# Windowed attention feeding an MoE-style block on one Trainium2 core: a written-out list of due times, and a planner that counts transfers

## The chip, the cores and the metric

The kernel runs on one core of one Trainium2 chip. The core has TensorE (matmuls; PE in the profile, PEld for its weight loads), VectorE (DVE), ScalarE (ACT), GpSimd (POOL), SyncE (SP, which here only issues transfers), and 16 DMA engines that all queues share. Each engine has its own in-order instruction queue. The metric is device microseconds of one execution; lower is better.

## The reference, cut to what matters

Attention over q, k, v of shape (4 batches, 8 heads, 768 positions, 64 wide), in which a query sees the first 8 positions and the last 96, with a bias that falls with distance; then a block on the 3072 tokens of 512 values.

```python
scores = scale * q @ k.T                         # per head, scale 1/8
keep   = is_global | is_local                    # first 8 keys, or 0 <= i - j < 96
scores = where(keep, scores + bias, -1e9)        # bias = -slope[h] * distance
a      = exp(scores - max); a = a / sum(a)
x      = (a @ v) as (B*S, H*D)                   # 3072 x 512

h    = x @ w_in                                  # 512 -> 1024
solu = h * softmax(h)
ln   = (solu - mean) / sqrt(var + 1e-6) * g_ln
out  = ln @ w_out                                # 1024 -> 512, fp32
```

## The kernel before, in words

The work is cut into steps. A batch's attention goes by pairs of heads (4 pairs a batch). For each pair, `k` and `q` are loaded in fp32 (`load_rows`, L338 to L347), cast to fp16 on POOL (for batch 0 also on ACT; L515), transposed by TensorE into PSUM (L523, L528) and evicted into `kT` and `qT` (L544 to L556). Batches 0 and 1 load "big" rows, in which a partition takes several neighbouring positions, 2 KB of `k` or 1.5 KB of `q` in one run; batches 2 and 3 load one position per run, 256 B. The big form needs a reordering eviction. `v` is always loaded in 56-row chunks of 256 B rows (`load_v`, L366, four transfers a pair; batch 0 in two parts) and cast into `v16` (L401). The scores of a pair are made in two groups of columns: a bias matmul (L592) and the banded products (L603), then one exponential on ACT (L611).

For each half batch (384 queries) the sums of the exponentials come from matmuls with ones (L628), their logarithm and reciprocal from ACT (L636, L639). The reciprocal is split into two fp16 numbers (L644, L645: `rh`, `rx`), spread over partitions by TensorE (L690), copied to SBUF (L696) and multiplied into the attention output (L673, in two turns) to give `xT` (L711).

The block has 24 tiles of 128 tokens. A tile is a product with `w_in` (L733), an exponential (L738) and a square (L745) on ACT with sums on the side, a product on DVE (L741), a transpose (L752) with its eviction into `uT` (L756, five buffers), and a product with the weights `gw_out_sb` (L787), scaled on ACT (L792) into one of four `osb` buffers and stored from SP's queue (L796). The statistics of three tiles are joined by four small DVE steps (L767 to L773) and two ACT steps (L777, L778). `gw_out_sb` is made once, from `w_out` scaled by `g` (L305, POOL), its mean by TensorE (L311) and a centring on DVE (L315).

The order on every engine is written out before the program is built. The class `Plan` is a list scheduler: a step names its engine, a duration, a due time (`target`), what it depends on, and a buffer that it takes or frees. Whenever an engine is free, the planner gives it the step with the smallest due time among those that are ready and whose buffer is there. The sequence of these decisions is the order of instructions. Due times before are formulas: batch 0 near 0 to 15, then a fixed pitch of `TT = 6.0` for each tile from `T0 = 21.0`. A transfer is an issuing step on a queue and a step of an engine called DMA, also picked by due time; any number of transfers can be under way between the two.

The lines that the prediction touches: L272 (`bias`), L245 to L302 (constants on POOL), L343 and L347 (issues of `k` and `q`), L366 (issues of `v`), L456 and L458 (`w_in`, `w_out`), L796 (stores).

## Time and profile before

| | |
|---|---|
| median of 3 runs | 228.91 us (228.6 to 230.17) |
| the profiled execution | 228.1 us, its span 226.3 us |
| TensorE busy | 168.1 us (74% of the span), granted clock 0.902 in the mean |
| VectorE busy | 132.6 us (59%) |
| ScalarE busy | 120.7 us (53%) |
| POOL busy | 58.6 us (26%) |
| moved by DMA | 29.20 MB in 59743 packets |

A page of the profile shows the busy share of each engine in 40 equal slices of the span, as digits in tenths. A row of a group has the line, the engine, the operation, output and inputs with shapes, how often, busy us and mean ns, and then the idle time of its engine just before with what ended it. A row in order of time has start and length in us; in brackets is the idle time before and its releaser. Clock is the share of full speed granted to TensorE. SPq, POOLq and ACTq are the queues' issuing instructions.

### The profile page before, as it was taken

The page shows a single profiled execution, that of the slowest core. Times are in us where ns is not written, and L with a number is a line of the kernel's source. Part 1 is how long each engine was busy: PE and PEld are TensorE (multiplying, and loading weights), DVE is VectorE, ACT ScalarE, POOL GpSimd, SP SyncE. Part 2 cuts the span into 40 slices and gives each one's busy share as a digit, 9 for nine tenths or more (in the row PEclk, how much of TensorE's full clock was granted, in tenths as well). Part 3 has the DMA queues.
Part 4 walks back from the last instruction along what each step waited for, and adds up shares of the span by engine and source line. Part 5 has one row for each costly group of instructions (what it writes and reads, how often), then busy time and mean ns, then how long its engine had stood idle before and what let it go on. Part 6 is the DMA issues. An engine that isn't in the chain of part 4 may idle for free.

```text
span 226.3 us, 5545 instructions
## 1 busy us (share of the span) xinstructions
PE 168.1 (74%) x2250; PEld 96.6 (43%) x2250; DVE 132.6 (59%) x276; ACT 120.7 (53%) x207; POOL 58.6 (26%) x118
## 2 busy tenths in 40 slices
PE   0249710038999696907999999979899996979993
PEld 0127510023566352403555646645565553354551
DVE  6997300168479869111477976576895547393550
ACT  2416920021395821307638769873868884572862
POOL 7794300034646953000230532113000000000000
PEclk9999985555699887995999999999999999997999
DMA  6995699649899999995667013121001112100113
GB/s 200 293 247 128 139 262 358 141 129 241 153 198 201 183 205 170 179 243 162 169 115 156 3 46 72 49 94 49 0 3 49 46 52 96 46 0 29 60 54 139
DMA packets 59743, 29.20 MB, mean 129 GB/s; under 512 B 51581, under 2 KB 54085, under 8 KB 59717
## 3 DMA queue, kind: packets, MB, share of 16 engines
q1 hardware_dynamic: 57572, 24.13, 46.9%
q0 software_dynamic: 1056, 3.15, 5.2%
q10 hardware_dynamic: 1088, 1.57, 2.3%
q8 instruction: 17, 0.28, 0.5%
q14 instruction: 10, 0.07, 0.1%
HBM read 23.14 MB, written 6.29 MB: 130 GB/s over the span
## 4 chain that ended last, share of the span: by engine, by line
PE 36%; DVE 8%; ACT 5%; SPq 4%; DMA 3%; issue 2%; ACTq 0%; DVEq 0%
PE ta L787 13%; PE big L733 10%; DMA out_dram<-osb 3%; PE ta L752 3%; ACT ef L738 2%; SPq L366 2%; PE ta L523 2%; PE big L592 2%; PE ta L673 2%; DVE uu L741 2%; PE ta L628 2%; DVE uT L756 2%; SPq L347 2%; PE big L603 1%; ACT osb L792 1%
## 5 line engine op out<-in xcount | busy, mean ns | idle before, releaser
L787 PE MATMUL ta<-gw_out_sb,uT 128*128 128x512 f16 x192 | 49.3, 408 | 0.1
L733 PE MATMUL big<-w_in_sb,xT 128*128 128x512 f16 x192 | 46.5, 393 | 1.4 <-DVE uu L741 1.4
L741 DVE SCALAR_TENSOR_TENSOR uu<-ef,big 128x1024 f16<-128x1024 f16 x24 | 29.2, 1218 | 21.4 <-ACT ef L738 21.3
L611 ACT ACTIVATE eb<-big 128x1008 f16<-128x1008 f32 x32 | 31.6, 1012 | 9.6 <-PE big L603 9.1
L738 ACT ACTIVATE ef<-big 128x1024 f16<-128x1024 f32 x24 | 24.5, 1021 | 14.7 <-PE big L733 14.5
L792 ACT ACTIVATE osb<-ta,rstd 128x512 f32<-128x512 f32 x24 | 16.4, 686 | 27.7 <-PE ta L787 14.8
L787 PEld LDWEIGHTS <-uT 128*128 128x128 f16 x192 | 19.1, 104 | 23.9 <-issue 6.8
L733 PEld LDWEIGHTS <-xT 128*128 128x128 f16 x192 | 18.8, 101 | 23.3 <-issue 4.8
L745 ACT ACTIVATE sq<-uu 128x1024 f16<-128x1024 f16 x24 | 25.3, 1053 | 2.9 <-DVE uu L741 2.9
L515 POOL CAST k<-k 96x1024 f16<-96x1024 f32 (+1 forms) x16 | 15.7, 987 | 29.4 <-issue 27.7
L401 POOL CAST v<-v 120x832 f16<-120x832 f32 (+2 forms) x20 | 15.0, 751 | 30.7 <-DMA v<-in_v_dram 29.3
L756 DVE COPY uT<-ta 128x1024 f16<-128x1024 f16 x24 | 16.2, 687 | 9.9 <-PE ta L752 9.9
L690 PE MATMUL ta<-rx,sel 32*128 32x384 f16 x32 | 5.8, 369 | 19.3 <-DVE rx L645 17.0
L673 PE MATMUL ta<-eb,v 64*64 64x152 f16 (+4 forms) x512 | 13.5, 227 | 5.9 <-DVE rb L696 2.6
L515 POOL CAST q<-q 128x768 f16<-128x768 f32 x14 | 12.0, 860 | 19.7 <-issue 19.5
L592 PE MATMUL big<-bias,ident 64*64 64x504 f16 (+2 forms) x160 | 13.8, 367 | 4.4 <-DVE uu L741 2.4
L523 PE MATMUL ta<-ident,q 128*128 128x128 f16 x96 | 9.4, 243 | 9.7 <-ACT q L515 9.7
L711 DVE TENSOR_TENSOR xT<-ta,rb 128x384 f16<-128x384 f32 x32 | 15.7, 548 | 0.3
L603 PEld LDWEIGHTS <-kT 64*64 64x64 f16 x480 | 13.6, 112 | 4.3 <-DVE kT L556 2.4
L401 DVE CAST v<-v 56x512 f16<-56x512 f32 (+1 forms) x8 | 3.6, 453 | 20.0 <-DMA v<-in_v_dram 19.9
L752 PE MATMUL ta<-ident,uu 128*128 128x128 f16 x192 | 15.0, 226 | 0.1
L603 PE MATMUL big<-qT,kT 64*64 64x152 f16 (+4 forms) x480 | 13.3, 226 | 1.9 <-DVE kT L556 1.9
(85 smaller groups left out, 202.2 us busy)
## 6 DMA issues: line engine op xcount, KB each, us to landing
k<-in_k_dram SPq DMA_DIRECT2D x16, 384.0 KB
out_dram<-osb SPq DMA_DIRECT2D x24, 256.0 KB
q<-in_q_dram SPq DMA_DIRECT2D x12, 384.0 KB
v<-in_v_dram SPq DMA_DIRECT2D x24, 98.0 KB
w_out<-in_moe_w_out_dram POOLq DMA_DIRECT2D x1, 2048.0 KB, 16.3
v<-in_v_dram SPq DMA_DIRECT2D x24, 84.0 KB
q<-in_q_dram ACTq DMA_DIRECT2D x4, 384.0 KB
w_in_sb<-in_moe_w_in_dram POOLq DMA_DIRECT2D x1, 1024.0 KB, 13.4
```

The costliest lines, as they stand in the source:

```text
L401: eng.tensor_copy(out=dst[rows, lo:hi, p, :], in_=src[rows, lo:hi, :])
L515: (nc.scalar.copy if ce == "ACT" else nc.gpsimd.tensor_copy)(**cast_rows(x16[cs["slot"]], x32[iss["slot"]], run)))
L603: nc.tensor.matmul(out=sc[o : o + 64, par, col : col + w], lhsT=kk[r, c, :], rhs=qq[r, q0 : q0 + w], start=False, stop=last[par] is pc, ti ...
L611: ex["fn"] = (lambda ex=ex, qk=qk: nc.scalar.activation(out=eb[ex["slot"]], in_=big_ps[qk["slot"]][:, :, 0:GC], func=AF.Exp, scale=inv_sqr ...
L733: nc.tensor.matmul(out=ph()[:, ts(fh, 512)], lhsT=xT[x_own["slot"]][:, j, ts(t % NA, P)], rhs=w_in_sb[:, j, ts(fh, 512)], start=(j == 0), ...
L738: ex["fn"] = lambda ex=ex, gidx=gidx, gcol=gcol, ph=ph: nc.scalar.activation(out=ef[ex["slot"]], in_=ph(), func=AF.Exp, accum_out=s0[gidx] ...
L741: u["fn"] = lambda u=u, ex=ex, gidx=gidx, gcol=gcol, ph=ph: nc.vector.scalar_tensor_tensor(out=uu[u["slot"]], in0=ef[ex["slot"]], scalar=U ...
L745: sqs["fn"] = lambda u=u, gidx=gidx, gcol=gcol: nc.scalar.activation(out=sq[0], in_=uu[u["slot"]], func=AF.Square, accum_out=s2[gidx][:, g ...
L752: nc.tensor.transpose(out=pt[:, ts(c, P)], in_=uu[u["slot"]][:, ts(c, P)], identity=ident)
L756: el["fn"] = lambda lt=lt, el=el: nc.vector.tensor_copy(out=uT[el["slot"]].rearrange("p c f -> p (c f)"), in_=ta_ps[lt["slot"]].bitcast(FP16))
L787: nc.tensor.matmul(out=ta_ps[g2["slot"]], lhsT=uT[el_x["slot"]][:, c, :], rhs=gw_out_sb[:, c, :], start=(c == 0), stop=(c == NFC - 1))
L792: ou["fn"] = lambda ou=ou, gidx=gidx, x=x, g2=g2: nc.scalar.activation(out=osb[ou["slot"]], in_=ta_ps[g2["slot"]], func=AF.Copy, scale=rst ...
```

## The change

Every step gets its due time from a list of 1105 numbers, `DUE`, one for each step in the order in which the program makes them, in tenths. The formulas still stand in the calls but are overwritten. In the planner the latency between engines is 0.08 in place of 0.15; a change of TensorE's tiling mode costs 0.11; steps of the engine DMA are served in the order in which they become ready; a transfer from SP or ACT holds one of eight `lane` places until it is done, and its data counts as there 1.2 us behind its end; many durations are changed.

Work that moves or changes:

- `w_out` is loaded from SP's queue in two halves instead of POOL's in one; the eight scalings of its rows go from POOL to ACT.
- `w_in` is issued from POOL behind the cast of pair 1's `k`, instead of behind `ident`.
- All four batches load big rows (`BIG_ROWS = 4`), and so use the longer evictions.
- The split of the reciprocal goes from DVE to POOL, as a tensor_scalar and a tensor_tensor.
- The statistics of three tiles go from four DVE steps to six POOL steps.
- `sel` and `negm` are made on DVE by seven steps instead of many on POOL; of `onesd` four small pieces are cleared instead of six set; two of the four `v32` buffers are cleared on POOL, and the clearing of `vt32` is replaced by that of 32 rows of the last chunk of `v16`.
- `v` of batch 0 comes in parts of seven and six chunks, and the fourteenth chunk apart; the spread of the first 8 rows (`spread_globals`) of later batches waits for the casts of `v`.
- Some dependencies are added among steps of one engine, so that their order is fixed (scores, turns of the attention output, tiles).

In the list, the due times (divided by 10) of the steps that the prediction speaks of are these. SP: the issues of batch 0's `k` -23.6 to -7.8, its own buffers taken at -27.7, -18.6, -16.6 and -8.4; the issues of batch 0's `v`, both parts, -33.4 to 0.0, one group opening at 3.7; `w_out` -1.1 and 1.3; the issues of batch 1's `k` 1.9, 4.9, 2.4 and 6.6, of which pair 1 takes its buffer at -11.1. POOL: `w_in` -8.7; the first split -8.4; the casts of the second part of batch 0's `v` -4.9 to -1.3. DVE: the evictions of batch 0's `kT` -16.6 to 16.3; `bias` 32.7, 24.0, 29.8 and 46.8.

The diff, cut to its core:

```diff
+DUE = [
+    -1234, -2098, -1472, -151, 1349, -1033, -1191, 432, 3269, 2400, 2983, 4677, -119, 1343, 85, -133, 1332, 229,
...
-    def step(self, eng, dur, target, deps, fn, take=None, free=None, lat=0.15):
+    def step(self, eng, dur, target, deps, fn, take=None, free=None, lat=0.08, mode=None):
         s = dict(eng=eng, dur=dur, target=target, deps=[d for d in deps if d is not None],
-                 fn=fn, take=(take, 1) if isinstance(take, str) else take, free=free or [], lat=lat, i=len(self.steps), slot=None)
+                 fn=fn, take=(take, 1) if isinstance(take, str) else take, free=free or [], lat=lat, mode=mode, i=len(self.steps), slot=None)
...
+        assert len(DUE) == len(steps)
+        for s, due in zip(steps, DUE):
+            s["target"] = due / 10.0
...
-                    heapq.heappush(waiting[s["eng"]], (s["target"], i))
+                    heapq.heappush(waiting[s["eng"]],
+                                   (now if s["eng"] == "DMA" else s["target"], i))
...
+                    if s["mode"] is not None:
+                        end += 0.11 if s["mode"] != mode[e] else 0.0
+                        mode[e] = s["mode"]
...
+    def constants_sel():
+        nc.vector.tensor_scalar(out=r31, in0=ri[:], scalar1=31, scalar2=None,
+                                op0=ALU.bitwise_and)
+        nc.vector.tensor_scalar(out=rodd, in0=ri[:], scalar1=1, scalar2=None,
+                                op0=ALU.bitwise_and)
+        nc.vector.tensor_scalar(out=negm, in0=rodd, scalar1=-1.0, scalar2=None, op0=ALU.mult)
+        nc.vector.tensor_scalar(out=two, in0=r31, scalar1=2.0, scalar2=None, op0=ALU.is_lt)
+        nc.vector.tensor_scalar(out=four, in0=r31, scalar1=4.0, scalar2=two, op0=ALU.is_lt,
+                                op1=ALU.subtract)
+        nc.vector.tensor_copy(sel[:, 0:64], two.to_broadcast([P, 64]))
...
     def weight_rows(j):
-        nc.gpsimd.tensor_scalar(out=gw_out_sb[:, j, :], in0=w_out32[:, j, :],
-                                scalar1=g32[:, j : j + 1], scalar2=0.0,
-                                op0=ALU.mult, op1=ALU.add)
+        nc.scalar.activation(out=gw_out_sb[:, j, :], in_=w_out32[:, j, :], func=AF.Copy,
+                             scale=g32[:, j : j + 1])
...
+    BIG_ROWS = 4
+    W_AT = 1
...
     def constants_zero():
-        for t in v32:
+        for t in v16:
+            for lo in (32, 96):
+                nc.vector.memset(t[lo : lo + 32, NBK - 1], 0.0)
+
+        for t in v32[0:2]:
             nc.vector.memset(t[32:64], 0.0)
-        nc.vector.memset(vt32[32:64], 0.0)
-        nc.vector.memset(vt32[96:128], 0.0)
-
-    zero_st = step("DVE", 1.6, -50.0, [], constants_zero)
-    first_st = step("POOL", 0.4, -50.0, [], constants_first)
-    pool_st = step("POOL", 0.6, -49.0, [], constants_pool)
-    glob_st = step("POOL", 3.2, -48.0, [], constants_global)
+
+    def constants_rows():
+        for t in v32[2:4]:
+            nc.gpsimd.memset(t[32:64], 0.0)
+
+    first_st = step("POOL", 0.5, -50.0, [], constants_first)
...
-
-    def load(fn, n_iss, us, target, deps, eng="SP", **kw):
-        iss = step(eng, 0.42 * n_iss, target, deps, None, lat=0.0, **kw)
-        iss["fn"] = lambda: fn(iss)
-        dma = step("DMA", us, target, [iss], None, lat=2.0)
-        return iss, dma
-
-    def pool_load(fn, us, target, deps):
-        iss = step("POOL", 0.9, target, deps, fn, lat=0.0)
-        return step("DMA", us, target, [iss], None, lat=2.0)
+    ones_st = step("POOL", 1.0, 8.0, [], constants_late)
+    sel_st = step("DVE", 1.0, 8.0, [pool_st], constants_sel)
+
+
+    def load(fn, us, target, deps, eng="SP", take=None, n=1):
+        own = step(eng, 0.0, target, deps, None, lat=0.0, take=take)
+        iss = own
+        for i in range(n):
+            iss = step(eng, 0.9 if eng == "POOL" else 0.42, target, [iss], None, lat=0.0,
+                       take="lane" if eng != "POOL" else None)
+            if i == 0:
+                iss["fn"] = lambda: fn(own)
+            dma = step("DMA", us / n, target, [iss], None, lat=1.2,
+                       free=[iss] if eng != "POOL" else None)
+        return own, dma
 
     _, gd_st = load(lambda i: nc.sync.dma_start(
-        out=g8, in_=moe_g_ln.rearrange("(j p) -> j p", p=P)), 1.0, 0.1, 6.0, [])
...
-    w_in_st = pool_load(lambda: nc.gpsimd.dma_start(
-        out=w_in_sb, in_=moe_w_in.rearrange("(j p) f -> p j f", p=P)), 5.6, 2.35, [first_st])
-    w_out_dma = pool_load(lambda: nc.gpsimd.dma_start(
-        out=w_out32, in_=moe_w_out.rearrange("(j p) c -> p j c", p=P)), 6.2, 34.5, [])
-    _, vgd_st = load(lambda i: load_globals(), 4, 0.5, 1.9, [])
-    vg_st = step("DVE", 0.5, 4.0, [vgd_st], cast_globals)
-    _, rest_st = load(lambda i: load_rests(), 2, 1.4, 12.0, [zero_st])
-    wr_st = [step("POOL", 0.7, 18.0 + 0.1 * j, [w_out_dma, g_st], lambda j=j: weight_rows(j))
+    w_out_dma = []
+    for i in range(2):
+        half = slice(NFC // 2 * i, NFC // 2 * (i + 1))
+        w_out_dma.append(load(lambda o, half=half: nc.sync.dma_start(
...
+    wr_st = [step("ACT", 0.6, 18.0 + 0.1 * j, [w_out_dma[2 * j // NFC], g_st], lambda j=j: weight_rows(j))
...
+            for part, lo, hi in ((0, 0, 7), (1, 7, NBK - 1)) if b == 0 else ((0, 0, NBK - 1),):
+                tv = 2.0 + 0.1 * p + 8.0 * part if b == 0 else base - 6.0 + 0.95 * TT * p
+                _, dma = load(lambda i, b=b, p=p, lo=lo, hi=hi, own=own:
+                              load_v(v32[own["slot"]], b, p, lo, hi),
+                              0.145 * (hi - lo) + 0.1, tv, [own], n=4)
+                tc_ = 10.0 + 0.1 * p + 8.0 * part if b == 0 else base + 2.5 + 0.95 * TT * p
+                for ce, rows in (("POOL", top), ("DVE", low)) if b == 0 else (("POOL", both),):
+                    cv = step(ce, (0.075 if ce == "POOL" else 0.053) * (hi - lo) + 0.08, tc_,
+                              [dma, vi], None)
+                    copy = nc.gpsimd.tensor_copy if ce == "POOL" else nc.vector.tensor_copy
...
+        own, gsd = load(lambda i, vi=vi, b=b: spread_globals(v16[vi["slot"]], b), 1.2,
+                        3.0 if b == 0 else base + 15.0,
+                        [cg[min(b, 1)], vi] + (v_st[0] if b else [zero_st]), n=2)
+        v_st[0].append(gsd)
+        v_st[1].append(gsd)
...
+                if b == 0 and p == W_AT and nm == "k":
+                    w_in_st = load(lambda o: nc.gpsimd.dma_start(
+                        out=w_in_sb, in_=moe_w_in.rearrange("(j p) f -> p j f", p=P)),
...
-            xs = step("DVE", 0.8, tS + 2.2, [re, late_st], None, take="rx", free=[re])
+            xs = step("POOL", 1.3, tS + 2.2, [re, sel_st], None, take="rx", free=[re])
 
             def split(xs=xs, re=re):
-                nc.vector.tensor_copy(rh[0], rr[re["slot"]])
-                nc.vector.scalar_tensor_tensor(out=rx[xs["slot"]], in0=rh[0], scalar=negm,
-                                               in1=rr[re["slot"]], op0=ALU.mult, op1=ALU.add)
+                nc.gpsimd.tensor_scalar(out=rh[0], in0=rr[re["slot"]], scalar1=negm, scalar2=0.0,
+                                        op0=ALU.mult, op1=ALU.add)
+                nc.gpsimd.tensor_tensor(out=rx[xs["slot"]], in0=rh[0], in1=rr[re["slot"]],
+                                        op=ALU.add)
             xs["fn"] = split
...
+
             def stats(gidx=gidx):
                 a, c = va[gidx], rstd[gidx]
-                nc.vector.scalar_tensor_tensor(out=a, in0=s1[gidx], scalar=-1.0 / D_FF / D_FF,
-                                               in1=s1[gidx], op0=ALU.mult, op1=ALU.mult)
-                nc.vector.scalar_tensor_tensor(out=a, in0=s2[gidx], scalar=1.0 / D_FF, in1=a,
-                                               op0=ALU.mult, op1=ALU.add)
-                nc.vector.scalar_tensor_tensor(out=c, in0=s0[gidx], scalar=eps, in1=s0[gidx],
-                                               op0=ALU.mult, op1=ALU.mult)
-                nc.vector.tensor_tensor(out=a, in0=a, in1=c, op=ALU.add)
-            st = step("DVE", 0.7, tt + 5.7, [x[1] for x in sts], stats)
+                nc.gpsimd.tensor_scalar(out=a, in0=s1[gidx], scalar1=-1.0 / D_FF, scalar2=0.0,
+                                        op0=ALU.mult, op1=ALU.add)
+                nc.gpsimd.tensor_tensor(out=a, in0=a, in1=s1[gidx], op=ALU.mult)
+                nc.gpsimd.tensor_tensor(out=a, in0=a, in1=s2[gidx], op=ALU.add)
+                nc.gpsimd.tensor_scalar(out=c, in0=s0[gidx], scalar1=eps * D_FF, scalar2=0.0,
+                                        op0=ALU.mult, op1=ALU.add)
+                nc.gpsimd.tensor_tensor(out=c, in0=c, in1=s0[gidx], op=ALU.mult)
+                nc.gpsimd.tensor_tensor(out=a, in0=a, in1=c, op=ALU.add)
+            st = step("POOL", 0.8, tt + 5.7, [x[1] for x in sts], stats)
 
...
-                so = step("SP", 0.4, tg + 2.5, [ou], None, lat=0.0)
-                so["fn"] = lambda ou=ou, x=x: nc.sync.dma_start(
-                    out=out[ts(x, P), :], in_=osb[ou["slot"]])
-                sd = step("DMA", 0.7, -50.0, [so], None, free=[ou], lat=2.0)
+                load(lambda o, ou=ou, x=x: nc.sync.dma_start(
```

More of the change, by code (lines that the diff above doesn't have):

```diff
@@ L62, in order @@
         busy = {e: 0.0 for e in waiting}
+        mode = {e: None for e in waiting}
         out = []
@@ L116, in order @@
         assert len(out) == len(steps)
-        self.end = max(s["start"] + s["dur"] for s in out)
+        self.end = max(busy.values())
         return out
@@ L223 @@
     dc10 = spare[:, 8 * WIN : 10 * WIN]
-    cr, isg, notg = many(3, [P, 1], FP32, "r_")
+    cr, isg, notg, two, four = many(5, [P, 1], FP32, "r_")
+    r31, rodd = many(2, [P, 1], I32, "ri_")
     HALVES = (slice(0, 64), slice(64, 128))
@@ L700 @@
                     if pp == 1:
-                        av2["free"].append(vi)
+                        step("PE", 0.0, ta0 + 1.6 * pp + 0.2, list(av_last.values()), None, free=[vi])
             for p in range(NPR):
```

359 lines of the change are left out of this document (171 added, 188 removed), and 60 rows, old and new, of the table DUE.

## The prediction

> **What bounds the kernel now.** I read the page's head and slices first, then busy time by stretches, then the order of time around the empty stretch.
>
> ```profile
> span 226.3 us, 5545 instructions
> PE   0249710038999696907999999979899996979993
> DMA  6995699649899999995667013121001112100113
> ```
>
> The slices are 5.66 us each. TensorE is dense (9) from about 57 us on, and nearly empty from 28 to 45 us and at 96 to 102 us, where the DMA row is full. In the table of stretches the columns are length, busy us of PE, PEld, DVE, ACT, POOL, the granted TensorE clock, the DMA share and GB/s.
>
> ```profile
> 0.00:4.00 4.00, 0.00 (x0) 0.00 (x0) 2.66 (x4) 0.78 (x1) 2.98 (x17) 1.00 0.46 148
> 4.00:16.00 12.00, 4.11 (x36) 2.71 (x36) 11.18 (x25) 3.67 (x5) 10.42 (x43) 1.00 1.09 282
> 30.60:44.40 13.80, 0.00 (x0) 0.00 (x0) 0.00 (x0) 0.00 (x0) 0.00 (x0) 0.58 0.94 269
> 54.80:96.00 41.20, 36.57 (x420) 20.22 (x419) 29.22 (x55) 20.00 (x34) 20.99 (x27) 0.85 1.05 184
> 96.00:103.70 7.70, 0.35 (x4) 0.16 (x4) 0.69 (x1) 1.63 (x3) 0.00 (x0) 0.83 0.84 188
> 108.00:220.00 112.00, 105.14 (x1428) 59.89 (x1427) 73.13 (x158) 77.79 (x141) 13.73 (x17) 0.98 0.21 60
> 54.80:222.60 167.80, 148.84 (x1893) 83.22 (x1891) 104.02 (x216) 103.25 (x184) 34.73 (x44) 0.93 0.46 101
> 64.00:72.00 8.00, 7.34 (x158) 5.20 (x158) 6.59 (x15) 6.45 (x10) 2.79 (x5) 1.00 1.04 202
> ```
>
> For 13.8 us no engine computes at all while the DMA engines are 94% busy. Behind that, TensorE is the bound: 148.84 of 167.8 us. Now the order of time around the gap:
>
> ```profile
> 25.62 0.69 SPq L343 DMA_DIRECT2D k<-in_k_dram  x1
> 26.58 0.92 POOL L458 DMA_DIRECT2D w_out<-in_moe_w_out_dram  x1
> 28.83 0.52 ACT L639 ACTIVATE rr<-lns 128x384 f32<-128x384 f32 x1
> 30.12 18.10 SPq L366 DMA_DIRECT2D v<-in_v_dram  x16
> 44.40 0.48 DVE L401 CAST v<-v 56x320 f16<-56x320 f32 x1 [15.77 <-DMA v<-in_v_dram]
> 45.41 0.62 DVE L645 SCALAR_TENSOR_TENSOR rx<-rh,negm,rr 128x384 f16<-128x384 f16 x1
> 46.08 0.51 PE L690 MATMUL ta<-rx,sel 32*128 32x384 f16 x4 [17.02 <-DVE rx L645]
> 54.83 3.59 PE L733 MATMUL big<-w_in_sb,xT 128*128 128x512 f16 x8
> ```
>
> The reciprocals of batch 0's first half end at 29.35 us. The split (L644, L645) that turns them into matmul operands stands on VectorE behind a cast of the second part of `v`. That `v` is asked for from 30.12 us on, behind loads of batch 1 and `w_out`, and lands at 44.4. So the 14 us are an order of transfers, passed on through VectorE's in-order queue. The first MoE matmul waits until 54.83 us.
>
> ```profile
> 98.38 0.38 SPq L796 DMA_DIRECT2D out_dram<-osb  x1
> 102.07 0.69 ACT L792 ACTIVATE osb<-ta,rstd 128x512 f32<-128x512 f32 x1 [9.60 <-DMA out_dram<-osb]
> ```
>
> The 7.7 us hole is of the same kind: ScalarE waits 9.6 us for an `osb` buffer whose store SP issued only at 98.38, behind loads.
>
> **The change part by part.** The sum is made on the profiled execution: 228.1 us, 226.3 of them span, 1.8 outside; the median of the runs shown, 228.91, lies 0.8 above it.
>
> *Order of loads.* In the new list (value ÷ 10, smallest first among what is ready) SP's loads of batch 0's `k` and of both parts of its `v` have issue values from -33.4 to 0 (one group opens at 3.7); `w_out` has -1.1 and 1.3, batch 1's `k` 1.9 to 6.6. The planner now serves transfers in the order they are issued, with eight places, so it counts a load behind another as late. `w_out` leaves POOL's queue for SP's, as two issues (0.4 us each, the 0.38 us of L796), behind batch 0's `v`; that puts no more than 0.8 us before batch 1's loads. `w_in` goes on POOL after the cast of pair 1's `k`. The constants that are dropped or moved between VectorE and POOL run in the first 4 us, before data is there, so I book nothing for them but the earlier casts below.
>
> *The start.* The first half of batch 0 needs `k` and `q` (2 x 8 heads x 768 rows x 256 B = 3.1 MB), seven of `v`'s fourteen chunks (0.8 MB) and, for the MoE, `w_in` (2.1 MB). At the rates above, 4 us x 148 GB/s bring 0.6 MB, and the rest at 282 GB/s takes 11.7 us without `w_in`, 19.2 with it: landed at 15.7 to 23.2 us. POOL and VectorE were late too:
>
> ```profile
> 10.36 5.95 DVE L272 TENSOR_SCALAR bias<-xT,sl 128x304 f16<-128x304 f32 x8
> 11.68 3.45 POOL L515 CAST k<-k 96x1024 f16<-96x1024 f32 x3
> 16.23 0.96 DVE L552 COPY kT<-ta 128x784 f16<-128x784 f16 x1
> 148.31 0.48 DVE kT L552
> L544 DVE COPY qT<-ta 128x768 f16<-128x768 f16 x4 | 3.8, 947 | 2.3 <-PE ta L523 2.3
> L548 DVE COPY qT<-ta 128x768 f16<-128x768 f16 x8 | 4.4, 550 | 1.5 <-PE ta L523 1.3 <-PE big L603 0.2
> ```
>
> POOL's first `k` cast waited until 11.68 us behind constants, of which `sel` and `negm` go to VectorE; the first `kT` eviction waited behind `bias`, which the list now puts last (24 to 46.8 against at most 16.3). From the last data to the reciprocals I estimate 6.4 us: cast 1.15 (a third of 3.45), eviction 0.96, and transposes, scores, exponential, sums, logarithm and reciprocal at some 0.7 each, between the 0.51 of L690 and the 0.96. From there to the first MoE matmul are the split, a broadcast, a copy, the attention output in two turns and a product, at 0.5 to 1.3 each: 4 us if they follow closely. Before, they took 9.42 (45.41 to 54.83), at half clock and with `v` casts between. So the first MoE matmul comes between 15.7 + 10.4 = 26 and 23.2 + 6.4 + 9.4 = 39, say 40 us; I take 31, near the lower, since `w_in` is asked for before batch 1.
>
> *Engines.*
>
> ```profile
> L644 DVE CAST rh<-rr 128x384 f16<-128x384 f32 x8 | 4.0, 504 | 9.4 <-ACT rr L639 9.3
> L645 DVE SCALAR_TENSOR_TENSOR rx<-rh,negm,rr 128x384 f16<-128x384 f16 x8 | 6.3, 782 | 0.3
> L767 DVE SCALAR_TENSOR_TENSOR va<-s 128x3 f32<-128x3 f32 x8 | 2.1, 266 | 0.1
> L773 DVE TENSOR_TENSOR va<-va,rstd 128x3 f32<-128x3 f32 x8 | 2.2, 280 | 0.3
> L305 POOL TENSOR_SCALAR gw_out_sb<-w_out,g 128x512 f16<-128x512 f32 x8 | 5.4, 688 | 0.0
> L298 POOL TENSOR_SCALAR_AFFINE_SELECT negm<-negm 4x1 f32<-4x1 f32 x8 | 2.0, 250 | 0.5
> L792 ACT ACTIVATE osb<-ta,rstd 128x512 f32<-128x512 f32 x24 | 16.4, 686 | 27.7 <-PE ta L787 14.8 <-DMA out_dram<-osb 10.9 <-issue 1.1
> ```
>
> VectorE loses the splits (10.3 us) and the statistics (four groups of eight, L767 first and L773 last, at most 32 x 0.28 = 9, I take 8), and gains, since batches 2 and 3 now load long rows, 8 x (0.96 - 0.48) + 8 x (0.947 - 0.550) = 7 us of slower evictions. In the dense stretch it is 73.13/112 busy, so I value this at nothing; TensorE's queue hides it, and without that cover it is a gain of 11 us (10.3 + 8 - 7). On POOL the first op of the split costs 688 x 384/512 = 0.52 us. No two-input POOL op is in the trace; as one more such pass it is 0.5, as POOL's longest cast 1.15. I take VectorE's own 0.78, which lies between: 1.3 a split against 1.29 before, nothing in sum, bounds -0.3 to +0.4 each, -2 to +3 for eight. Behind it on POOL wait casts of the next batch; POOL is 13.73 of 112 us busy there, so they have cover. The statistics' six tiny ops are at most 6 x 0.25 = 1.5 us (L298) against 1, and less if POOL is quicker at them; the output matmul runs meanwhile, so nothing. The eight weight rows move to ScalarE, 8 x 0.7 = 5.5 us by L792's row of this width; ScalarE is 77.79/112 busy, nothing on the path unless `w_out` comes late.
>
> The Trainium skill (GPSIMD Engine Reference, Engine selection) says a two-input elementwise op is about twice as slow there as on VectorE, which speaks against moving the split; by it the second op takes 1.56 us and the sum would be up to 6 us longer. No run shown here has the op.
>
> *Long rows.* `k` and `q` of batches 2 and 3, 6.3 MB at 202 GB/s (64 to 72 us, short rows) is 31 us of transfers, at 282 it is 22. That falls in 54.8 to 103.7, where DMA is full; I book it as the hole at 96 closing.
>
> *The dense stage.* TensorE's 148.84 us contain half-clock time:
>
> ```profile
> 52.00:56.00 4.00, 3.71 (x30) 1.74 (x30) 3.08 (x7) 0.96 (x2) 1.46 (x2) 0.50 1.15 233
> 56.00:60.00 4.00, 4.00 (x15) 1.85 (x14) 1.69 (x4) 1.11 (x2) 2.67 (x3) 0.50 0.82 135
> ```
>
> At the later stretch's clock they are 148.84 x 0.93/0.98 = 141; I take 145, as not every pause goes. The first 60 us at the density of 54.8 to 96 (36.57/41.2 = 0.888) hold 53.3 of work, the other 91.7 at 105.14/112 = 0.939 take 97.7: 157.7 us. Bounds: 141.2/0.939 = 150.4 and 148.84/0.888 = 167.6.
>
> The Trainium skill (TensorE: Matmul & The Clock Gate, Part 1) has the full clock back after about 3.4 us of sustained work. The rows above disagree: 7.7 us of work at 0.50. By the rule each pause would cost less and the credit for clock, 4 us, would be about half.
>
> *The end.* From 222.6 to 226.3 us is 3.7: a last scale and store, kept.
>
> Sum: 31 + 157.7 + 3.7 + 1.8 = 194.2, plus 0.8 to a median: **195 us**. By the bounds, the split's -2 and +3 in them: 26 + 150.4 + 6.3 - 2 = 181, and 40 + 167.6 + 6.3 + 3 = 217.
>
> **The rivals.** *The weights become the wait.* `w_out` took 16.3 us to land before:
>
> ```profile
> w_out<-in_moe_w_out_dram POOLq DMA_DIRECT2D x1, 2048.0 KB, 16.3
> 81.23 5.36 DVE L315 SCALAR_TENSOR_TENSOR gw_out_sb<-w_out,g,ta 128x512 f16<-128x512 f32 x8 [2.22 <-PE ta L311]
> ```
>
> Issued near 24 us it is there at 40; rows 5.5, the mean at most 3.6 (eight 512-wide matmuls, as at 54.83) and centring 5.4 make 54. Five `uT` buffers and batch 1's attention cover that stretch; if it lands 10 us later TensorE pays most of it, also because batch 1's exponentials stand behind the waiting weight row on ScalarE: about 206.
>
> *The change does not do what it says.* A `k` of batch 1 takes one of four `k32` buffers early (value -11.1, before batch 0's last at -8.4); if loads of batch 1 again stand before `v` on the chip, the 13.8 us stay and only the second hole (7.4) and some 5 us of the start go: 228.9 - 12 = 216.
>
> *Slower: the split behind POOL's casts.*
>
> ```profile
> POOL v L401 <- DMA v<-in_v_dram: 29.3, 9, 17.1
> ```
>
> POOL waited 29.3 us for `v` in nine waits, 17.1 the longest, and is in-order. The split, now on POOL, comes before every half batch's attention output, and TensorE stands behind its broadcast (17.02 us at 46.08). Eight passes: at (228.9 - 195)/8 = 4.2 us exposed each, nothing is left of the gain; at 5 us it is 235. Against it: behind 108 us the DMA share is 0.21, so later casts find their data.
>
> **How the numbers follow.** Forecast (181 to 206) 0.62; weights 0.14; front stays 0.10; slower 0.09; better than the lower bound 0.05. The range 182 to 216 takes in the bounds but for their last microsecond, and leaves out the slower case, the better one and about half of the 216 case. What a measurement can tell from no change is about 1%: the cases below 226.6 hold 0.91, of which I move 0.03 to within 1%; slower 0.09.
>
> **What would show it.**
>
> ```profile
> DMA packets 59743, 29.20 MB, mean 129 GB/s; under 512 B 51581, under 2 KB 54085, under 8 KB 59717
> ```
>
> First MoE matmul (the `big<-w_in_sb,xT` group) at 26 to 40 us; no stretch over 4 us without work behind 20 us; no `osb` wait for a store over 3 us; packets under 512 B (51581 above) down by 2 batches x 2 x 8 heads x 768 rows = 24576; the dense stage at 0.9 or more. It is wrong if the first MoE matmul still starts behind 45 us, if POOL's waits for `v` show as TensorE's waits for `rx`, or if the dense stage has new holes from its own order.

## The result, and the profile after

The changed kernel takes 196.66 us (median of 4 runs, 193.41 to 197.94), the kernel before 229.19 us (228.6 to 230.17) beside it: a ratio of 0.849, 95% interval 0.838 to 0.860. Ratios and intervals here compare the shorter, undisturbed runs of both kernels alone (195.89 and 193.41 us of these four), so they differ a little from the quotients of the medians. The prediction was 195 us. The profiled execution took 195.89 us, 194.1 of them span.

The page's head and slices of the changed kernel (a slice is now 4.85 us):

```profile
span 194.1 us, 5568 instructions
PE   0375617998399989969799999999999999999992
PEclk9999556669979999999999999999999999999998
DMA  5988946589999999979999954311000121011222
DMA packets 39278, 29.19 MB, mean 150 GB/s; under 512 B 27021, under 2 KB 31573, under 8 KB 39253
```

The empty stretch of 28 to 45 us is gone, and so is the hole near 100. What is left of the front is one slice with a 1 (24 to 29 us). Behind it stands one 3 (49 to 53 us, where TensorE waits 2.17 us for a cast of `k` on POOL); from 53 us on no slice of TensorE is below 6, and from 97 us on all but the last are 9. The bytes are the same, in fewer packets: 51581 - 27021 = 24560 fewer short ones.

Busy us by stretches of the changed kernel, with the prediction's columns (length, PE, PEld, DVE, ACT, POOL, clock, DMA share, GB/s):

```profile
22.50:28.40 5.90, 0.26 (x4) 0.00 (x0) 1.77 (x3) 0.47 (x1) 1.06 (x2) 0.50 0.69 138
39.00:64.00 25.00, 21.44 (x221) 10.99 (x222) 19.62 (x38) 16.37 (x29) 9.18 (x19) 0.86 1.02 229
64.00:112.00 48.00, 44.22 (x779) 27.94 (x777) 34.75 (x61) 35.06 (x57) 30.14 (x46) 1.00 1.00 230
112.00:188.00 76.00, 75.25 (x908) 40.77 (x907) 44.74 (x83) 56.44 (x106) 13.87 (x41) 1.00 0.18 62
39.00:190.30 151.30, 143.15 (x1913) 80.53 (x1913) 99.12 (x180) 108.56 (x192) 53.19 (x105) 0.98 0.58 144
```

Behind 112 us TensorE is busy 75.25 of 76 us: nothing is left to gain there, except by doing some of this work earlier. Between 39 and 64 us it misses 3.6 us, between 64 and 112 us 3.8.

In order of time around what is left of the front gap:

```profile
14.39 0.34 SPq L415 DMA_DIRECT2D k<-in_k_dram  x1
14.82 12.48 SPq L438 DMA_DIRECT2D v<-in_v_dram  x12
26.61 0.62 DVE L472 CAST v<-v 56x448 f16<-56x448 f32 x1 [8.53 <-DMA v<-in_v_dram]
27.24 0.97 DVE L659 COPY kT<-ta 128x784 f16<-128x784 f16 x1
28.45 0.63 PE L691 MATMUL big<-qT,kT 64*64 64x152 f16 x14 [5.69 <-DVE kT L663]
38.91 3.59 PE L827 MATMUL big<-w_in_sb,xT 128*128 128x512 f16 x8
```

The pattern is that of before, shorter: SP reaches the load of pair 3's `k` only at 14.39 us, among parts of `v`; VectorE waits 8.53 us for `v`, and the eviction of pair 3's `kT`, which TensorE needs, stands behind that cast. So the first MoE matmul is at 38.91 us, against 54.83.

The second product, which needs the finished weights, by its tile in both kernels (count, shortest, median and longest ns, first and last start in us), the kernel before and then the changed one:

```profile
L305 POOL TENSOR_SCALAR gw_out_sb<-w_out,g x8: 683/688/692, 70.2 to 74.9; 128x512 f16<-128x512 f32 x8
L787 PE MATMUL ta<-gw_out_sb,uT x192: 376/379/634, 87.2 to 222.1; 128*128 128x512 f16 x192
```

```profile
L378 ACT ACTIVATE gw_out_sb<-w_out,g x8: 707/710/712, 43.6 to 52.1; 128x512 f16<-128x512 f32 x8
L883 PE MATMUL ta<-gw_out_sb,uT x192: 379/379/390, 62.6 to 189.9; 128*128 128x512 f16 x192
```

It starts at 62.6 us and not at 87.2. The prediction did not ask what sets the 87.2: the weights' rows came only at 70.2 there, though `w_out`, issued at 26.58 with 16.3 us to land, was in by 43. Together with the two waits that the prediction named, that makes three, and the experiments ask what each of them is worth.

### The profile page after: what moved, and what is told of

It is laid out like the page before. It is cut to its first block, busy times and chain, and to the rows that moved or that the text cites. A ratio compares the mean times of both kernels' runs of the same rounds, so it can differ in the third digit from the quotient of the medians.

```text
span 194.1 us, 5568 instructions
## 1 busy us (share of the span) xinstructions
PE 163.1 (84%) x2266; PEld 94.5 (49%) x2266; DVE 122.3 (63%) x238; ACT 126.1 (65%) x215; POOL 73.1 (38%) x154
## 2 busy tenths in 40 slices
DMA packets 39278, 29.19 MB, mean 150 GB/s; under 512 B 27021, under 2 KB 31573, under 8 KB 39253
## 4 chain that ended last, share of the span: by engine, by line
PE 54%; DMA 22%; POOL 6%; issue 5%; DVE 4%; SPq 4%; ACT 3%; ACTq 1%; POOLq 0%; DVEq 0%
PE big L827 18%; PE ta L883 16%; DMA v<-in_v_dram 13%; DMA q<-in_q_dram 6%; PE ta L766 5%; PE ta L846 4%; SPq L438 3%; DMA k<-in_k_dram 3%; PE ta L783 3%; PE ta L630 2%; PE big L680 2%; PE big L691 2%; PE ta L717 1%; POOL rx L735 1%; POOL k L617 1%
## 5 line engine op out<-in xcount | busy, mean ns | idle before, releaser
L883 PE MATMUL ta<-gw_out_sb,uT 128*128 128x512 f16 x192 | 44.6, 379 | 0.0
L827 PEld LDWEIGHTS <-xT 128*128 128x128 f16 x192 | 17.7, 99 | 20.3 <-issue 2.5
L883 PEld LDWEIGHTS <-uT 128*128 128x128 f16 x192 | 17.9, 98 | 19.8
L617 POOL CAST k<-k 96x1024 f16<-96x1024 f32 x16 | 16.9, 1060 | 16.9 <-DMA k<-in_k_dram 9.9
L472 POOL CAST v<-v 120x832 f16<-120x832 f32 (+2 forms) x20 | 14.5, 737 | 14.0 <-DMA v<-in_v_dram 13.9
L691 PE MATMUL big<-qT,kT 64*64 64x152 f16 (+4 forms) x480 | 14.4, 237 | 5.7 <-DVE kT L663 5.7
L691 PEld LDWEIGHTS <-kT 64*64 64x64 f16 x480 | 14.5, 120 | 8.5 <-DVE kT L663 6.1
L659 DVE COPY kT<-ta 128x784 f16<-128x784 f16 x16 | 15.5, 969 | 4.9 <-PE ta L635 4.7
L789 DVE COPY rb<-ta 128x384 f32<-128x384 f32 x16 | 8.7, 555 | 12.2 <-PE ta L783 12.2
L862 POOL TENSOR_SCALAR va<-s 128x3 f32<-128x3 f32 x8 | 1.6, 195 | 36.3 <-DVE uu L835 36.2
L680 PE MATMUL big<-bias,ident 64*64 64x504 f16 (+2 forms) x160 | 14.8, 384 | 0.3 <-ACT eb L699 0.3
## 6 DMA issues: line engine op xcount, KB each, us to landing
w_in_sb<-in_moe_w_in_dram POOLq DMA_DIRECT2D x1, 1024.0 KB, 12.8
```

What stands on the lines that cost most here:

```text
L617: (nc.scalar.copy if ce == "ACT" else nc.gpsimd.tensor_copy)(**cast_rows(x16[cs["slot"]], x32[iss["slot"]], run)))
L680: nc.tensor.matmul(out=sc[o : o + 64, par, c0_:c1_], lhsT=ident[r, r], rhs=bias[r, p, at : at + c1_ - c0_], start=(i == 0), stop=False, ti ...
L691: nc.tensor.matmul(out=sc[o : o + 64, par, col : col + w], lhsT=kk[r, c, :], rhs=qq[r, q0 : q0 + w], start=False, stop=last[par] is pc, ti ...
L827: nc.tensor.matmul(out=ph()[:, ts(fh, 512)], lhsT=xT[x_own["slot"]][:, j, ts(t % NA, P)], rhs=w_in_sb[:, j, ts(fh, 512)], start=(j == 0), ...
L883: nc.tensor.matmul(out=ta_ps[g2["slot"]], lhsT=uT[el_x["slot"]][:, c, :], rhs=gw_out_sb[:, c, :], start=(c == 0), stop=(c == NFC - 1))
```

## The experiments

Each kernel was timed beside the kernel before on one chip. The kernel before had a median of 227.79 us in the first group (the first four kernels below), 226.5 in the second (the changed kernel again and the three after it), 225.96 in the third (the last two, and the second measurement of the short rows with the changed kernel beside it). Profile rows come from one execution of each kernel.

**Only the front gap.** In the kernel before, the second part of batch 0's `v` takes a buffer of its own, and gets it late. Here both parts of a pair share one buffer.

```diff
+                own_v = held.get(p)
...
-                                load_v(v32[i["slot"]], b, p, lo, hi),
-                                4, 1.8 * (hi - lo) / NBK, tv, [zero_st], take="v32")
+                                load_v(v32[(own_v or i)["slot"]], b, p, lo, hi),
+                                4, 1.8 * (hi - lo) / NBK, tv, [zero_st, own_v],
+                                take=None if own_v else "v32")
...
```

> The kernel before with one edit: the two parts of batch 0's v of a pair share one v32 buffer, so that the second part's load need not wait for a buffer that the first part's cast frees. Its loads then stand ahead of batch 1's k and q on SP's queue. Theory (the gap is an order of transfers, made by four v32 buffers): the empty stretch 30.6 to 44.4 us shrinks below 5 us, the first MoE matmul comes at 38 to 46 us in place of 54.8, and the time is 212 to 220 us. Rival (the start is bound by what the DMA engines can bring, in whatever order): the first MoE matmul stays behind 50 us and the time at 225 us or more.

Measured 229.9 us (224.98 to 231.47; before 227.79), too scattered for a ratio: no gain can be seen, and the shortest run, 224.98, is no shorter than that of the kernel before, 224.61. The stretch that was empty, and its two products by their tiles:

```profile
30.60:44.40 13.80, 4.16 (x62) 2.08 (x62) 5.88 (x14) 1.84 (x4) 1.92 (x5) 0.51 0.85 215
L740 PE MATMUL big<-w_in_sb,xT x192: 376/379/634, 47.7 to 211.2; 128*128 128x512 f16 x192
L794 PE MATMUL ta<-gw_out_sb,uT x192: 376/379/634, 86.0 to 219.0; 128*128 128x512 f16 x192
```

And among its waits (sum in us, how many, the longest) that of ScalarE for a store:

```profile
ACT osb L799 <- DMA out_dram<-osb: 12.2, 3, 10.9
```

The gap is shorter but not closed: TensorE works 4.16 of the 13.8 us. The first MoE matmul came 7.1 us earlier (47.7 against 54.8; the theory had 38 to 46), the second product 1.2 us (86.0 against 87.2), and the wait for a store stayed (10.9 us the longest, 9.6 before). The theory that the front gap alone holds most of the time has fallen: the 7 us that are won there are given back at the next wait, where the weights' rows come at 70.5 us as before. The rival, DMA engines that cannot bring the data sooner in any order, has the time but not the place (behind 50 us).

**Only the planner's account of transfers.** The kernel before with the new rules for the engine DMA, the eight places and the 1.2 us, and formulas for due times as before.

```diff
-                    heapq.heappush(waiting[s["eng"]], (s["target"], i))
+                    heapq.heappush(waiting[s["eng"]],
+                                   (now if s["eng"] == "DMA" else s["target"], i))
...
+            iss = step(eng, 0.42, target, [iss], None, lat=0.0, take="lane")
...
+            dma = step("DMA", us / n_iss, target, [iss], None, lat=1.2, free=[iss])
...
```

> The kernel before with only the planner's new account of transfers (served in the order in which they are issued, eight places for SP and ACT, there 1.2 us behind their end), due times by formula as before, all work where it was. Theory (buffers, not the planner's account, put v behind): the gap stays, 222 to 232 us. Rival (the planner's account alone finds the order): the gap closes and the time is 205 to 216 us.

Measured 217.72 us, ratio 0.964 (0.951 to 0.976). That is less time than the theory gave, and a little more than its rival's range. With this account the planner puts other work first, as the tiles of the weights and the two products show:

```profile
L738 PE MATMUL big<-w_in_sb,xT x192: 376/379/631, 40.6 to 204.6; 128*128 128x512 f16 x192
L306 POOL TENSOR_SCALAR gw_out_sb<-w_out,g x8: 682/682/686, 36.9 to 46.2; 128x512 f16<-128x512 f32 x8
L792 PE MATMUL ta<-gw_out_sb,uT x192: 376/379/634, 60.3 to 212.4; 128*128 128x512 f16 x192
```

Its wait for stores:

```profile
ACT osb L797 <- DMA out_dram<-osb: 15.6, 6, 7.2
```

The first MoE matmul is at 40.6 and the second product at 60.3 us, both about where the changed kernel has them. The third wait, that for a store, has grown from 10.9 to 15.6 us in sum, in six pieces of at most 7.2.

**The changed kernel without its list.** All else as changed, due times by the formulas that still stand in the calls.

```diff
-        assert len(DUE) == len(steps)
-        for s, due in zip(steps, DUE):
-            s["target"] = due / 10.0
```

> The changed kernel without the list: due times by the formulas that still stand in the calls; planner, moved work, long rows and shared v buffers as changed. Theory (most of the gain is the shared buffers and the planner, the list adds the denser stage): first MoE matmul at 35 to 45 us, time 201 to 210 us. Rival (the list is what gains): 215 us or more. Rival (the list adds nothing): within 2 us of the changed kernel, 194 to 199 us.

Measured 207.82 us, ratio 0.921 (0.911 to 0.931), in the range of the theory. So the list is worth 11 to 16 us (by the ratio of 0.921 against 0.870 and 0.849 for the changed kernel in two groups), and the rest of the change 18 to 20. Where the list's share lies is read from the stretches of this kernel:

```profile
56.00:64.00 8.00, 2.87 (x32) 2.32 (x32) 7.21 (x12) 1.11 (x2) 3.90 (x5) 0.71 1.14 212
64.00:112.00 48.00, 43.45 (x690) 26.54 (x689) 28.18 (x50) 28.13 (x43) 26.51 (x36) 0.87 1.03 236
112.00:199.00 87.00, 82.11 (x1022) 45.20 (x1020) 49.13 (x90) 62.57 (x119) 15.50 (x47) 1.00 0.15 51
```

The start is no worse here (first MoE matmul at 35.0 us, second product at 64.0), but ahead of the second product TensorE stands still for 5.1 of 8 us, where the changed kernel is busy all 8. From 64 to 112 us TensorE is as busy as with the list, but at clock 0.87 and with 690 matmuls in the trace where the list's order has 779 at 1.00. So behind 112 us there are 82.11 - 75.25 = 6.9 us more work left, and 87 - 82.11 = 4.9 us of pauses instead of 0.75. Over the whole dense stage, from the first MoE matmul to the end of the last second product, this execution has 148.85 us of work in 165.4 (clock 0.94), the changed kernel 143.25 in 151.4 (0.98): 5.6 us of work and 8.4 us of pauses more, less the 3.9 us by which it starts earlier, which is the 10.2 us between the two spans (204.3 and 194.1) to within 0.1. Which of the 1105 numbers bring this was not separated.

**Short rows again in batches 2 and 3**, the order kept as the list makes it.

```diff
-                n, run = run if big else NA, run if big else 0
+                long_ = b < 2
+                n, run = run if long_ else NA, run if long_ else 0
...
```

> The changed kernel with its order of instructions kept, but k and q of batches 2 and 3 loaded in 256 B rows with the short evictions, as before. Theory (long rows are worth some 9 us of transfers while DMA is full): DMA stays full some 9 us longer, TensorE gets new waits for k behind 70 us, time 199 to 206 us. Rival (hidden): within 1.5 us of the changed kernel, since the evictions get 7 us shorter and TensorE does not wait.

Measured 198.87 us, ratio 0.882 (0.874 to 0.890): a little under the theory's range, and 2.2 us above the 196.66 of the changed kernel, a little over the rival's 1.5. It was measured once more in the third group, with the changed kernel beside it:

> Short rows in batches 2 and 3 in the changed kernel once more, now beside the changed kernel itself on the same chip. Theory (long rows are worth 2 to 4 us, since TensorE has new waits of some us behind 78 us): 1 to 2% slower than the run beside it. Rival: within 0.5%.

> The changed kernel itself, as the measure for the short rows: 193 to 198 us.

199.18 us (196.81 to 200.22), ratio 0.882 (0.876 to 0.888), against 196.3 us (194.49 to 198.19), ratio 0.870 (0.864 to 0.877), for the changed kernel. The medians are 2.9 us apart (1.4% by the ratios, as the theory had it), and the intervals overlap by a hair. A stretch of the kernel with short rows, its wait for stores, and the same stretch of the changed kernel:

```profile
64.00:112.00 48.00, 41.52 (x735) 26.59 (x734) 27.30 (x55) 32.05 (x51) 24.34 (x37) 0.96 0.98 205
```

```profile
ACT osb L889 <- DMA out_dram<-osb: 2.9, 1, 2.9
```

```profile
64.00:112.00 48.00, 44.93 (x782) 28.29 (x780) 35.30 (x63) 35.67 (x59) 30.13 (x47) 1.00 1.02 236
```

Both move data all the time (shares 0.98 and 1.02), the short rows at 205 GB/s and the long ones at 236. With the short rows TensorE gets 3.4 us less done in this stretch. But the longest wait for a store is 2.9 us: the hole at 96 does not come back with them.

**The changed kernel again**, as the measure for the next two.

> The changed kernel itself once more, as the measure for the two runs beside it: 193 to 198 us.

195.3 us (193.41 to 196.6), ratio 0.864 (0.848 to 0.880).

**Split and statistics on VectorE**, in the places that the list gives them on POOL's step.

```diff
-                nc.gpsimd.tensor_tensor(out=rx[xs["slot"]], in0=rh[0], in1=rr[re["slot"]],
-                                        op=ALU.add)
+                nc.vector.scalar_tensor_tensor(out=rx[xs["slot"]], in0=rh[0], scalar=negm,
+                                               in1=rr[re["slot"]], op0=ALU.mult, op1=ALU.add)
...
```

> The changed kernel with its order kept, but the split of the reciprocal and the statistics issued on VectorE as in the kernel before (the same places in the order of steps). Theory (they cost nothing on either engine, TensorE's queue hides them): within 1.5 us of the changed kernel beside it. Rival (POOL's two-input op of 0.92 us is on the way of every half batch): 2 to 5 us faster. Rival (VectorE is near its limit): 3 us or more slower.

198.61 us (197.1 to 202.6), ratio 0.880 (0.870 to 0.889). The median is 3.3 us (1.7%) higher, and the intervals of the two overlap widely. That is on the side of the second rival, a VectorE near its limit: it points to a gain of 0 to 4 us from the move to POOL, and settles no more than that the move does not cost the 4 to 5 us a pass that the prediction's slower rival needed.

**What is left of the front gap.** In the changed kernel, VectorE's casts of the first part of `v` are moved behind the eviction of pair 3's `kT`; nothing else.

```diff
...
+    moved = [s for s in made if s["i"] in late]
+    made = [s for s in made if s["i"] not in late]
+    at = [s["i"] for s in made].index(evk_last["i"]) + 1
+    made[at:at] = moved
```

> The changed kernel with one move in VectorE's order: the casts of the first part of batch 0's v that stand ahead of the eviction of pair 3's kT go behind it. In the changed kernel VectorE waits 8.53 us for v there, and pair 3's scores wait with it. Theory (that wait is on the path to the first MoE matmul, but the attention output needs the same v, so only the work between can move up): the first MoE matmul comes 3 to 6 us earlier, the time 1 to 4 us shorter. Rival (v sets the start anyway, or the gain is given back where the weights are waited for until 62 us): within 1 us.

194.51 us (193.53 to 196.02), ratio 0.864 (0.855 to 0.873) against 0.864 for the changed kernel in the same group: the same, so the theory's 1 to 4 us did not come and the rival's range did. Yet the gap was there and was closed. The stretch in the changed kernel of this group, and then the stretch, the order of time and the tiles of the edited kernel:

```profile
22.50:28.40 5.90, 2.36 (x57) 1.55 (x57) 3.45 (x6) 1.91 (x3) 1.06 (x2) 1.00 0.59 112
```

```profile
22.50:28.40 5.90, 4.67 (x124) 3.52 (x120) 2.21 (x4) 5.15 (x7) 1.87 (x4) 1.00 0.67 132
```

```profile
31.66 0.65 PE L771 MATMUL ta<-eb,v 64*64 64x152 f16 x13 [1.11 <-DMA v<-vg]
```

```profile
L832 PE MATMUL big<-w_in_sb,xT x192: 379/379/634, 35.5 to 176.4; 128*128 128x512 f16 x192
L888 PE MATMUL ta<-gw_out_sb,uT x192: 379/379/631, 59.6 to 188.6; 128*128 128x512 f16 x192
```

TensorE works 4.67 of the 5.9 us in which it had worked 2.36 beside it (0.26 in the execution shown above: the wait for `v` differs between executions, 5.1 and 8.5 us). It then meets the next thing that is late, the spread of the first rows of `v` (`v<-vg`). The first MoE matmul comes at 35.5 us, against 37.2, 38.6 and 38.9 in three executions of the changed kernel, so 1.7 to 3.4 us earlier where the theory had 3 to 6. Within the group the second product comes at 59.6 (61.1), and the spans are 192.8 and 193.0 us: the 2.3 us of work at the front come out as 1.7 and 1.5 us on the way and as 0.2 at the end.

**The two earlier waits together.** The kernel before, with shared buffers for `v` as above and an earlier due time for `w_out`.

```diff
-        out=w_out32, in_=moe_w_out.rearrange("(j p) c -> p j c", p=P)), 6.2, 34.5, [])
+        out=w_out32, in_=moe_w_out.rearrange("(j p) c -> p j c", p=P)), 6.2, 12.0, [])
...
```

> The kernel before with two edits: the shared v buffers of the first run, and the due time of w_out's load 12.0 in place of 34.5, by which the planner puts the scaling of the weights 10 steps earlier on POOL. Theory (the earlier start of the first run was given back because the second product could not start before 86 us, its weights being scaled at 70): the second product starts at 55 to 68 us, and the time is 212 to 221 us. Rival (the store that waits behind loads near 96 us, or DMA that is full until 110 us, sets the time, whatever comes before): 226 us or more.

224.46 us, ratio 0.998 (0.993 to 1.002). The theory had the place right and the time wrong: the second product starts at 67.3 us, within its 55 to 68 and 20 us earlier than before, but the time is 3.5 us above its range, and the ratio shows no gain. The mechanism of the rival, a wait for a store that takes the gain, came out (its 226 us or more is missed by 1.5). From 82 to 95 us this kernel stands still, as the stretch and the order of time show:

```profile
82.40:95.50 13.10, 0.01 (x1) 0.01 (x1) 0.00 (x0) 0.75 (x2) 0.88 (x1) 0.59 1.00 191
```

```profile
89.58 1.82 SPq L803 DMA_DIRECT2D out_dram<-osb  x1
94.75 0.69 ACT L799 ACTIVATE osb<-ta,rstd 128x512 f32<-128x512 f32 x1 [16.55 <-DMA out_dram<-osb]
95.49 1.86 PE L794 MATMUL ta<-gw_out_sb,uT 128*128 128x512 f16 x4 [14.17 <-ACT osb L799]
```

For 13.1 us next to no matmul runs. The tiles come earlier, the loads of the later batches stand on SP's queue where they stood, and a store is issued only at 89.58; ScalarE waits 16.55 us for its buffer, TensorE 14.17 behind it.

**All three.** The same kernel, with its stores issued from POOL's queue.

```diff
-                so["fn"] = lambda ou=ou, x=x: nc.sync.dma_start(
+                so["fn"] = lambda ou=ou, x=x: nc.gpsimd.dma_start(
```

> The kernel before with three edits: shared v buffers, the due time 12.0 of w_out's load, and the stores issued from POOL's queue in place of SP's (same places in the order of steps), so that no store stands behind loads. Theory (three waits in series, each of which takes up what the one before it gives: v, then the weights, then an osb buffer whose store stands behind loads): the hole of 12 us near 84 to 95 closes, ScalarE waits less than 4 us in all for osb buffers, and the time is 206 to 215 us. Rival (DMA that is full until 110 us sets the time): 220 us or more.

214.69 us (213.88 to 214.89), ratio 0.955 (0.950 to 0.960), in the theory's range. The stretch of the hole, and the wait for stores:

```profile
84.00:96.00 12.00, 9.62 (x185) 5.80 (x184) 6.85 (x18) 8.96 (x15) 5.18 (x7) 1.00 1.06 223
```

```profile
ACT osb L799 <- DMA out_dram<-osb: 7.6, 5, 2.4
```

The stretch that was empty has 9.62 us of work in 12, and no wait for a store is over 2.4 us; their sum, 7.6 us, is above the 4 that the theory allowed. The first two edits alone gave 0.2%, with the third 4.5%. The front gap is shortened here and not closed: the first MoE matmul comes at 46.3 us, the second product at 67.5.

**Only the stores.** The kernel before with that third edit alone.

> The kernel before with the third edit alone: stores issued from POOL. Theory: the hole at 96 to 103 closes, but the first MoE matmul stays at 55 and the second product at 87 us; 218 to 225 us. Rival (the store is what counts, the other two nothing): within 2 us of the run with all three.

220.58 us (218.29 to 223.01), ratio 0.978 (0.971 to 0.986), in the theory's range. The front gap stays (first line; the first MoE matmul comes at 56.0 us, the second product at 84.8), and the hole at 96 is closed (second):

```profile
30.00:44.00 14.00, 2.05 (x70) 1.63 (x66) 0.17 (x1) 2.60 (x5) 0.00 (x0) 0.62 1.00 285
96.00:104.00 8.00, 7.80 (x95) 3.73 (x95) 2.86 (x6) 5.12 (x11) 3.28 (x5) 0.79 1.15 265
```

These two rows are of an execution of 223.01 us, the longest of the four, and serve for where the holes are and not for the sum. ScalarE still waits for stores, 8.1 us in all, but at most 4.7 at once (10.9 and 9.6 before).

## Why the prediction was right, point by point

The sum, 195 us, was off by 1.7 us, but two of its terms were off by more, against each other.

**The first MoE matmul: 31 us taken, bounds 26 to 40; it came at 38.9.** It was the largest miss, 8 us. The step that failed is "landed at 15.7 to 23.2 us", which divides the bytes by a rate of 282 GB/s. The last of the data was there at 26.7 us (`w_in`, issued at 13.9 and 12.8 us on its way; VectorE's cast of the `v` that it waited for starts at 26.61). The stretch until then, and the piece of the chain of work that ends at that cast:

```profile
16.00:26.70 10.70, 4.42 (x82) 3.11 (x81) 2.17 (x7) 4.53 (x5) 1.03 (x1) 0.62 0.91 169
15.73 10.79 DMA v<-in_v_dram
```

The stretch moves 169 GB/s at a share of 0.91, not 282. A transfer of `v` whose issue had ended by 15.73 us took 10.79 us (the second row has start and length), with `w_in` under way at the same time. The 31 us had the data at 20.6 and 10.4 us for the chain behind it; that chain took 38.9 - 26.7 = 12.2. So some 6 us of the miss are the landing and 2 the chain, whose estimate left out that VectorE's queue again puts an eviction behind the wait for `v`. So "no stretch over 4 us without work behind 20 us" was wrong too (0.26 of 5.9 us). The upper bound held only because it had the slow chain of before in it (6.4 + 9.4 us, where 12.2 came).

**The dense stage: 157.7 us taken, bounds 150.4 to 167.6; it took 151.3.** It is 6.4 us shorter and has the mechanism that was argued, with both sizes better: 143.15 us of work where 145 was taken, at a density of 0.946 where 145/157.7 = 0.919 was. For the work the credit for a better clock was 4 us; it fell by 148.84 - 143.15 = 5.7. That the clock is the cause fits the other traces: in this stage the kernel without the list has 148.85 us of work at clock 0.94, the kernel with the later casts 145.7 at 0.96, the changed kernel in its three executions 143.2 to 143.5 at 0.98 and 0.99. The prediction's estimate from the rule of the Trainium skill (TensorE: Matmul & The Clock Gate, Part 1) was about half of that credit; the trace does not agree. For the density the first part ran at (21.44 + 44.22)/73 = 0.899 (0.888 taken for 60 us), and the part from 112 us on at 75.25/76 = 0.990. That last one was the miss: 0.939, the density of the kernel before, was carried over as if it were a limit of the stage, though the prediction's own row showed no engine there that would set it.

**The end and what lies outside**: 3.8 and 1.8 us against 3.7 and 1.8, and 0.8 from the profiled execution to the median, as taken; this last is chance, since the four executions lie between 193.41 and 197.94 us. With the first two: 38.9 + 151.3 + 3.8 + 1.8 = 195.8.

The start and the dense stage are not the independent terms that the sum made of them. In the kernel with the later casts the first came 1.7 us sooner, and the end only 0.2 us: its dense stage took 1.6 us more (153.5 against 151.9), with 2.2 us more work at a clock of 0.96 in place of 0.98. Whether the earlier start brings that, or the execution, is open. That the two misses of the sum cancel is luck as far as the runs show.

**The reading of before.** The prediction explained the time before by the front gap and the hole at 96, and gave the long rows the credit for closing the second ("I book it as the hole at 96 closing"). Both steps are too simple. The three waits stand in series: `v` behind loads of batch 1; the weights' rows late on POOL; a store behind loads on SP. Shortening the first gives nothing that can be measured, the first and second 0.2%, closing the third alone 2.2%, all three 4.5%. (The planner's account, which eases the first two as well and leaves no wait for a store over 7.2 us, gives 3.6%.) The hole is one of order on SP's queue, as the prediction's row of it said: with short rows it does not return, with stores on another queue it goes at once. The long rows are worth 2 to 3 us, and not by the hole.

**POOL's split: 1.3 us taken with -0.3 to +0.4; it took 1.50.** The rows of the changed kernel:

```profile
L733 POOL TENSOR_SCALAR rh<-rr,negm 128x384 f16<-128x384 f32 x8 | 4.7, 584 | 18.8 <-ACT rr L728 18.8
L735 POOL TENSOR_TENSOR rx<-rh,rr 128x384 f16<-128x384 f16 x8 | 7.3, 919 | 0.7
L862 POOL TENSOR_SCALAR va<-s 128x3 f32<-128x3 f32 x8 | 1.6, 195 | 36.3 <-DVE uu L835 36.2
```

And TensorE's wait for it:

```profile
PE ta L783 <- POOL rx L735: 0.8, 2, 0.5
```

584 and 919 ns, where 520 and 780 were booked. The statistics' first op is 195 ns, the other five 193 to 196; all six are 1.2 us, under the 1.5 booked. TensorE waited 0.8 us for `rx` in all, which is the end of the slower rival (it needed over 4.2 us in each of eight passes). That VectorE's relief is worth nothing is less sure: with this work back on VectorE the median was 3.3 us higher. In the kernel that keeps this work on VectorE, the op that does the same takes 727 ns, so POOL's two-input op is 919/727 = 1.26 times as long. The Trainium skill (GPSIMD Engine Reference, Engine selection) puts that at about twice; the trace does not agree for this op.

**The front as a rival.** The gap did not stay, but up to 5.9 of its 13.8 us did, in another place and for a part of `v` that comes earlier; by the kernel with the later casts they cost next to nothing.

**The weights.** The rival had them ready at 54 us, and 10 us later if `w_out` landed late. The rows ran from 43.6 to 52.1, the mean from 53.6, the second product from 62.6. So its delay of 8 to 9 us did happen, but its price did not: TensorE is 21.44 of 25 us busy in 39 to 64, a loss of 3.6 us at most where the rival booked nearly all of the 10. Attention of the next batch covered the rest, as the forecast said. The rows took 710 ns each, 5.2 us of ScalarE's time in all, where 5.5 was booked.

**Packets and stores.** 24560 short packets fewer, 24576 predicted; one wait for a store, of 1.7 us (under 3 predicted):

```profile
ACT osb L888 <- DMA out_dram<-osb: 1.7, 1, 1.7
```

**What the parts are worth.** The planner's account of transfers alone gives 3.6%; with the moved work, the shared buffers of `v` and the long rows, by formula, 7.9%; with the list 13 to 15%, as the three groups measured it. Inside the last, one execution of each shows the place (fewer pauses, from 56 us on, and less work at a better clock) and not the cause: which due times bring it is open, and so is how the second part divides between moved work, buffers and long rows.

## What to carry to other kernels

Look for the waits in series before pricing one of them: take each stage's first instruction from the trace, ask what it waits for and what would be late next, and follow that to the end, since easing one wait here gave 0 to 2% and three gave 4.5%. A store that shares an in-order queue with loads was late here as soon as the tiles came early; check that queue first when work is pulled forward. Bytes over the best rate of another stretch gave too early a landing here (282 GB/s taken, 169 found): take the rate of the stretch in question, and ask which other transfers are under way beside the one that is waited for. And compare several executions of one kernel before a single profile is given a cause.

## What the runs showed of the hardware

TensorE's clock can stay at half speed while it works. Stretches of the changed kernel, with a faster one among them:

```profile
28.00:32.00 4.00, 3.54 (x82) 2.51 (x82) 2.07 (x5) 2.75 (x4) 0.09 (x1) 0.50 0.61 122
32.00:36.00 4.00, 2.65 (x78) 1.74 (x76) 1.25 (x3) 2.80 (x6) 3.10 (x6) 0.93 0.45 106
36.00:40.00 4.00, 3.90 (x48) 1.99 (x40) 3.25 (x7) 0.96 (x2) 2.56 (x4) 0.50 0.90 286
40.00:42.00 2.00, 2.00 (x6) 0.59 (x4) 1.07 (x3) 0.00 (x0) 0.00 (x0) 0.50 0.88 138
```

3.54 and 3.90 of 4 us busy at clock 0.50, and 0.93 in between with only 2.65 busy: the clock does not follow the work of the same stretch. The Trainium skill (TensorE: Matmul & The Clock Gate, Part 1) has full speed back after about 3.4 us of sustained work; the rows of 36 to 42 us, with 5.90 of 6 us of work at 0.50, do not agree.

The gap at 22.5 to 28.4 us is not what brought the low clock: it was 0.50 already from 20 us on, ahead of the gap. In the kernel with the later casts, which closes the gap, the clock is 1.00 from 22.5 to 28.4 us and again 0.50 from 32 to 40. And in the changed kernel of the third group, with the same order of instructions and a shorter wait at the gap (2.75 us of TensorE against 5.69), the clock was 1.00 all the way from 20 to 48 us, here in the stretch that had 0.50:

```profile
36.00:40.00 4.00, 3.89 (x38) 1.91 (x30) 3.53 (x7) 0.96 (x2) 2.22 (x4) 1.00 0.99 276
```

So one program can run the same stretch at half or at full clock, and what decides it is open. It cost little here: the first MoE matmul came at 38.6 us in that execution and at 38.9 in the one at half clock.
